# A written-out order replaced in a linear-attention and FFN kernel, with tiny copies placed between its loads

## The chip, the cores and the metric

One NeuronCore of one Trainium2 chip runs the program; the other cores are idle. The time is the device time of one execution in microseconds (us). An execution has five instruction streams: TensorE (PE; its weight loads are the row PEld), VectorE (DVE), ScalarE (ACT), GpSimd (POOL) and SyncE (SP), which here only issues transfers (DMAs). Each runs its own instructions in order and waits on semaphores for the others.

## What is computed

The first half is a chunked linear attention with decay over 4 batches, 8 heads, 768 tokens, head width 32 and state width 16; the second is a layer norm and a two-layer FFN (width 256, inner width 1024) with a residual.

```python
L = np.exp(cum[:, :, :, None] - cum[:, :, None, :]) * causal    # cum: running sum of log(a) in the chunk
y_intra = np.einsum('bhij,bhjd->bhid', (C B^T) * L, xc)
y_inter = np.einsum('bhin,bhnd->bhid', Cc, state) * np.exp(cum)[..., None]
state = decay_full * state + sum_j(B_j x_j * decay_from_j)
...
xn = (y - mean) / np.sqrt(var + 1e-06) * g_ln
out = y + np.maximum(xn @ w_ch1, 0.0) @ w_ch2
```

The weights arrive as 64-bit words and are turned into float32 on the chip, and then into an upper and a lower part of type fp32r, so that three fp32r products stand for one float32 product.

## The kernel before

The 768 tokens are cut into six blocks `t` of 128 tokens; a block holds all four batches, so a hidden tile has 512 columns. Every step of a block is a small function (a "layer"), called with the block and sometimes a group, half, batch or slice. The whole program is one list, `ISSUE` (from line 560): a text of short names with numbers, written out by hand or by a tool, in which each piece calls one function through the table `do` (line 543). The instructions of each engine run in the order of that list; a suffix (`:v`, `:a`, `:p`) puts a step on DVE, ACT or POOL, where the function's default would be another engine. Loads (`ld`) and stores (`od`) are all issued by SP in that order too. A buffer of a pool is given out in the order of the list, and the engine that writes it waits until the readers of its last content are done.

The names that matter here:

- Loads: `ld la` (the decays a), `ld sums`, `ld c t`, `ld b t`, `ld bt t`, `ld x t`, `ld as` (a in another layout), `ld g`, four quarters of W1 (`ld w1 c k`, 512 KB each: inner columns `c`, input rows `k`), four of W2 (`ld w2 c`), `ld mask`, `ld id`, `ld sel`.
- Decays of blocks 0 and 1: `l1`, `l2` (clip and logarithm), `e`, `x` (sums to the end of the chunk, exp), `lr`, `dc`, `du` (logarithms repeated, running sums on PE, exp into `u` and `d`), `so`, `sm`, `mb`, `sp`, `em` (sums of the sub-blocks, spread over the partitions).
- Decays of blocks 2 to 5: `rcl`, `ru`, `riv`, `rd` (two scans on DVE over `as`), `ro` (two writes of the result to a scratch tensor `scr` in HBM, line 322), `ld ud t` (loads of it, line 141).
- Attention of a block: `C`, `cx`, `cm` (C scaled and parted by head parity), `B` (B scaled), `ones` and `W` (mask and decays in `WW`), `G` (scores on PE, L375), `R` (scores times `WW`, L381), `be`, `Z`, `K`, `S`, `sb` (state of the half blocks), `c2`, `Vi` (product with the state, L394), `V` (product with x, L402), `y` (result to SBUF), `T`, `tc` (transposed), `yh`, `yl` (upper and lower part), `st`, `ag`, `rs`, `rc` (statistics).
- Weights: `k0` (ACT), `k1`, `k2`, `k3` (DVE), `kr` (ACT), `f` (sum of two integers, on POOL or DVE): words to float32; `gm` (centring matrix `gd`, `gneg` from g), `wc` (centring of W1 on PE, L230), `wh`, `wl` (upper and lower part).
- FFN: `h t m` (a hidden group, six products of 512 columns, L489), `hh` (relu and upper part), `hl` (lower part, DVE), `o t b` (24 products of 256 columns, L507), `oc 0 c j` (the same work of block 0 cut in four parts, L517), `oe` (scale and residual, DVE), `od` (store, 128 KB).
- `fill i n`: a product of zeros with n columns (L534), which computes nothing.

PSUM has eight banks: five for the attention (`ps_att`), three for `h`, `o`, `wc` and the sums (`ps_ffn`). Output tiles `o` come from a pool with three buffers. The hidden tiles `hh` and `hl` have nine buffers each.

```python
def load(what, *at, e=nc.sync):
    ...
    W1[at] = p1.tile([P, 1024], I32, tag=f"w1{c}{k}", name=f"raw1{c}{k}")
    e.dma_start(W1[at], w1v[k * P:(k + 1) * P, c * 1024:(c + 1) * 1024])
def finished(t, b):
    o = tiles["o", t, b] = p3.tile([P, DM], F32, tag="o", name=f"o{t}{b}")
for piece in ISSUE.split(","):
    name, *at = piece.split()
    name, _, engine = name.partition(":")
    do[name](*(int(v) if v.isdigit() else v for v in at), **({"e": engines[engine]} if engine else {}))
```

## Time and profile before

| what | value |
|---|---|
| median of 3 runs | 202.52 us (200.40 to 204.73) |
| profiled execution | 199.18 us |
| its span, first to last instruction | 197.4 us |
| mean granted TensorE clock | 0.998 |
| busy: PE, PEld, DVE, ACT, POOL | 188.8, 162.5, 129.1, 69.3, 35.7 us |
| HBM read, written | 14.74 MB, 3.28 MB |

The trace is one profiled execution; all its times are counted from the start of its span. The time of that execution holds 1.8 us more than the span. A busy engine is one with an instruction in it; products of PE are pipelined and their ends modelled, so a row's length can overlap the next row's. The view that follows the chain of work back from the last instruction shows one piece behind the other without overlap.

### The profile page before, as it was taken

The numbers are of one execution on the slowest core, as the hardware profiler recorded it, in microseconds if no ns is written. First come the engines' busy times: TensorE is split into PE (matmuls) and PEld (weight loads), VectorE is DVE, ScalarE is ACT, GpSimd is POOL, SyncE is SP. The second block draws the span as 40 slices with busy tenths as digits, with TensorE's granted clock in tenths as the row PEclk, the third lists the DMA queues.
The fourth block names the chain that finished last, engine by engine and source line by source line (L and its number), as shares of the span: only waits on it lengthen the run. The fifth ranks groups of instructions, "written<-read, shape, count | busy, mean of one in ns | idle before, by whom it ended". The sixth has DMA issues, their size and how long they took to land.

```text
span 197.4 us, 6404 instructions
## 1 busy us (share of the span) xinstructions
PE 188.8 (96%) x2854; PEld 162.5 (82%) x2854; DVE 129.1 (65%) x273; ACT 69.3 (35%) x127; POOL 35.7 (18%) x41
## 2 busy tenths in 40 slices
...
GB/s 118 286 367 401 375 307 235 202 149 15 3 163 0 0 53 119 220 67 58 3 3 0 3 150 67 3 3 0 11 72 53 0 3 3 80 27 3 19 17 71
DMA packets 11660, 18.42 MB, mean 93 GB/s; under 512 B 2385, under 2 KB 5873, under 8 KB 11633
## 3 DMA queue, kind: packets, MB, share of 16 engines
...
q8 instruction: 22, 0.36, 0.8%
...
HBM read 14.74 MB, written 3.28 MB: 91 GB/s over the span
## 4 chain that ended last, share of the span: by engine, by line
PE 90%; DVE 3%; ACT 3%; DMA 2%; issue 1%; POOL 0%; DVEq 0%
PE ph L489 32%; PE po L507 29%; PE pp L517 5%; PE yps L402 4%; PE wc L230 4%; PE G L375 4%; PE idle L534 4%; PE yps L394 3%; PE yt L458 3%; PE Z L414 2%; DMA out_dram<-o 2%; DVE hl L500 1%; DVE o L522 1%; ACT y L441 1%; PE cum L271 1%
## 5 line engine op out<-in xcount | busy, mean ns | idle before, releaser
L507 PE MATMUL po<-w,hh 128*128 128x256 f32 x320 | 56.8, 281 | 0.1
L489 PE MATMUL ph<-yh,w 128*128 128x512 f32 x192 | 53.8, 402 | 0.5 <-DVE hl L500 0.5
L507 PEld LDWEIGHTS po<-w,hh 128*128 128x128 f32 x320 | 49.1, 188 | 1.0 <-DVE hl L500 0.4
L507 PE MATMUL po<-w,hl 128*128 128x256 f32 x160 | 44.7, 279 | 0.0
L494 ACT ACTIVATE hh<-ph 128x512 fp32r<-128x512 f32 x34 | 20.2, 598 | 68.7 <-PE ph L489 59.8
L489 PEld LDWEIGHTS ph<-yh,w 128*128 128x128 f32 x192 | 34.3, 188 | 7.9 <-DVE hl L500 0.8
L500 DVE SCALAR_TENSOR_TENSOR hl<-ph,hh 128x512 fp32r<-128x512 f32 x48 | 32.3, 683 | 11.4 <-ACT hh L494 11.2
L507 PEld LDWEIGHTS po<-w,hl 128*128 128x128 f32 x160 | 30.1, 188 | 0.0
L489 PE MATMUL ph<-yl,w 128*128 128x512 f32 x96 | 29.8, 392 | 0.0
L522 DVE SCALAR_TENSOR_TENSOR o<-po,rstd,ytok 128x256 f32<-128x256 f32 x20 | 9.5, 480 | 27.3 <-PE po L507 27.2
L489 PEld LDWEIGHTS ph<-yl,w 128*128 128x128 f32 x96 | 18.0, 188 | 4.2 <-DVE yl L450 0.3
L381 DVE TENSOR_TENSOR R<-G,WW 128x512 f32<-128x512 f32 x24 | 15.7, 677 | 2.4 <-PE G L375 2.4
L450 POOL TENSOR_TENSOR yl<-y,yh 128x512 fp32r<-128x512 f32 x6 | 8.4, 1403 | 35.2 <-DVE yh L447 22.0
L496 DVE TENSOR_SCALAR hh<-ph 128x512 fp32r<-128x512 f32 x14 | 9.5, 681 | 4.9 <-PE ph L489 4.9
L441 ACT COPY y<-yps 128x256 f32<-128x256 f32 x15 | 5.2, 374 | 18.8 <-PE yps L402 15.1
L517 PE MATMUL pp<-w,hh 128*128 128x256 f32 x64 | 11.4, 281 | 0.0
L470 DVE BATCH_NORM_STATS2 st<-ytok 128x6 f32<-128x256 f32 x24 | 9.9, 416 | 1.4 <-ACT ytok L463 1.4
L517 PEld LDWEIGHTS pp<-w,hh 128*128 128x128 f32 x64 | 9.9, 188 | 0.3
L361 ACT COPY WW<-wt 32x1024 f32<-32x1024 f32 x8 | 8.3, 1040 | 5.1 <-DVE R L381 5.0
L534 PE MATMUL idle<-const-float32-0.0 128*128 128x128 f32 (+3 forms) x34 | 9.2, 425 | 0.8 <-PEq L624 0.8
L402 PE MATMUL yps<-R,xt 64*32 64x64 f32 x768 | 9.2, 226 | 0.0
L345 POOL TENSOR_TENSOR bs<-b,ud 128x512 f32<-128x512 f32 x3 | 3.9, 1293 | 28.6 <-DMA b<-in_bn_dram 28.6
...
## 6 DMA issues: line engine op xcount, KB each, us to landing
raw<-in_w_dram SPq DMA_DIRECT2D x8, 512.0 KB, 9.0
xt<-in_x_dram SPq DMA_DIRECT2D x6, 512.0 KB, 6.0
...
```

What stands on the lines that cost most here:

```text
L381: nc.vector.tensor_tensor(out=R.rearrange("p b i k -> p b (i k)"), in0=tiles.pop(("G", t, q)).rearrange("p b i k -> p b (i k)"), in1=WW.re ...
L402: nc.tensor.matmul(tiles["y", t, g, f][32 * k:32 * k + 32, b], x[r, b * NH + h], tiles["R", t, h // 2][r, b, h % 2], start=(t + f + b == 0 ...
L450: e.tensor_tensor(out=tiles["yl", t][:, g], in0=tiles["y32", t][:, g], in1=tiles["yh", t][:, g].bitcast(F32), op=ALU.subtract)
L470: nc.vector.bn_stats(out=st, in_=tiles["ytok", t][:, b])
L489: nc.tensor.matmul(ph, W1[m // 4, k][:, s, mc], v[:, k], start=(i == 0), stop=(i == len(cmb) - 1))
L494: e.activation(h, tiles["ph", t, m], AF.Relu)
L496: e.tensor_scalar(out=h, in0=tiles["ph", t, m], scalar1=0.0, scalar2=None, op0=ALU.max)
L500: nc.vector.scalar_tensor_tensor(out=l, in0=tiles.pop(("ph", t, m)), scalar=0.0, in1=tiles["hh", t, m].bitcast(F32), op0=ALU.max, op1=ALU. ...
L507: nc.tensor.matmul(po, tiles[v, t, m][:, cols], W2[m // 2,][:, s, (m % 2) * DM:(m % 2 + 1) * DM], start=(n == 0), stop=(n == len(cmb) - 1))
L517: nc.tensor.matmul(tiles["po", t, b], tiles[v, t, m][:, cols], W2[m // 2,][:, s, (m % 2) * DM:(m % 2 + 1) * DM], start=(c + n + b % 2 == 0 ...
L522: nc.vector.scalar_tensor_tensor(out=o, in0=tiles.pop(("po", t, b)), scalar=tiles["rstd", t][:, b], in1=tiles["ytok", t][:, b], op0=ALU.mu ...
L534: nc.tensor.matmul(ps[:, :n], zero.to_broadcast([P, P]), zero.to_broadcast([P, n]), start=True, stop=True)
```

## The change

Eight copies of 4 bytes (`pc`) are put between the loads. Each is issued by SP, reads the first element of a tile that is being loaded and writes it to a tile `seen` that nobody reads; so SP waits there until that load has landed. `gm`, a tile of g / 256, is left out, since `gneg` can be added instead of `gm` subtracted; the centring has a form for ACT, and so has `sb`. The output tiles get a pool of their own with six buffers, `rp` and `hp` one buffer more each. And the whole list `ISSUE` is a new one, with the same layers on the same data: 5 fills instead of 17; `ld w1 0 0` moved forward to fifth place, `ld as` and `ld g` moved back behind a copy; other engines for some steps (`be`, `c2`, `f` more often on POOL, `hh`, `y`, `yh`, `cm` more often on DVE, `sb` thrice on ACT, `ones` on POOL); and four hidden groups of block 0 (`h 0 1`, `0 2`, `0 0`, `0 3`) before the products `wc 1` of the second half of W1. The list is shown here by its opening in both versions, and by the end of the new one.

```diff
--- before.py
+++ after.py
@@ -88,8 +88,9 @@
     p1 = pool("p1", 1)
     p2 = pool("p2", 2)
     p3 = pool("p3", 3)
-    rp = pool("rp", 8)
-    hp = pool("hp", 9)
+    rp = pool("rp", 9)
+    hp = pool("hp", 10)
+    op = pool("op", 6)
 
     ov = out.rearrange("b (t p) f -> b t p f", p=P)
     w1v, w2v = w1.bitcast(I32), w2.bitcast(I32).rearrange("(m p) f -> p m f", p=P)
@@ -99,7 +100,6 @@
     cf = hp.tile([P, 4 * P], F32, tag="hl", name="cf")
     la = cp.tile([P, NT, NR], F32, name="la")
     gt = cp.tile([P, KC], F32, name="gt")
-    gm = cp.tile([P, KC], F32, name="gm")
     gneg = cp.tile([P, KC], F32, name="gneg")
     gd = hp.tile([P, KC, P], F32, tag="hh", name="gd")
     selt = cp.tile([NR, P + NB], F32, name="selt")
@@ -163,6 +163,13 @@
                 sums=(cf, coefs), g=(gt, g_ln), sel=(selt, sel))[what]
             e.dma_start(dst, src)
 
+    seen = cp.tile([1, 64], F32, name="seen")
+
+    def after(i, what, *at):
+        src = W1[at].bitcast(F32) if what == "w1" else W2[at].bitcast(F32) if what == "w2" else tiles[(what, *at)]
+        src = src.rearrange("p r d -> p (r d)") if what == "x" else src
+        nc.sync.dma_start(seen[:, 8 * i:8 * i + 1], src[:1, :1])
+
     epst = cp.tile([P, 1], F32, name="epst")
 
     def restart(e=nc.gpsimd):
@@ -218,11 +225,14 @@
         e.tensor_tensor(out=f, in0=f, in1=low.pop((w, *at)), op=ALU.add)
 
     def centring(e=nc.vector):
-
-        e.tensor_scalar(out=gm, in0=gt, scalar1=1.0 / DM, scalar2=None, op0=ALU.mult)
-        e.tensor_scalar(out=gneg, in0=gt, scalar1=-1.0 / DM, scalar2=None, op0=ALU.mult)
-        for k in range(KC):
-            e.tensor_scalar(out=gd[:, k], in0=ident, scalar1=gt[:, k:k + 1], scalar2=gm[:, k:k + 1], op0=ALU.mult, op1=ALU.subtract)
+        if e is nc.scalar:
+            e.activation(gneg, gt, AF.Copy, scale=-1.0 / DM)
+            for k in range(KC):
+                e.activation(gd[:, k], ident, AF.Identity, bias=gneg[:, k:k + 1], scale=gt[:, k:k + 1])
+        else:
+            e.tensor_scalar(out=gneg, in0=gt, scalar1=-1.0 / DM, scalar2=None, op0=ALU.mult)
+            for k in range(KC):
+                e.tensor_scalar(out=gd[:, k], in0=ident, scalar1=gt[:, k:k + 1], scalar2=gneg[:, k:k + 1], op0=ALU.mult, op1=ALU.add)
 
     def centred(c, k):
         w = centre[c, k] = ps_ffn.tile([P, 512], F32, tag="ffn", name=f"wc{c}{k}")
@@ -432,7 +442,12 @@
     def diagonal(t, f, e=nc.gpsimd):
 
         sb = tiles["sbd", t, f] = p2.tile([P, NB, 2 * HD], F32, tag=f"sbd{f}", name=f"sbd{t}{f}")
-        e.tensor_tensor(out=sb, in0=tiles[("S", *before(t, f))], in1=blkt.unsqueeze(1).to_broadcast([P, NB, 2 * HD]), op=ALU.mult)
+        S = tiles[("S", *before(t, f))]
+        if e is nc.scalar:
+            for i in range(2):
+                e.activation(sb[:, :, i * HD:(i + 1) * HD], S[:, :, i * HD:(i + 1) * HD], AF.Copy, scale=even[:, i:i + 1])
+        else:
+            e.tensor_tensor(out=sb, in0=S, in1=blkt.unsqueeze(1).to_broadcast([P, NB, 2 * HD]), op=ALU.mult)
 
     def gathered(t, g, f, e=nc.scalar):
         if ("y32", t) not in tiles:
@@ -518,7 +533,7 @@
                                  start=(c + n + b % 2 == 0), stop=(c == MC // 2 - 1 and b % 2 == 1 and n == len(cmb) - 1))
 
     def finished(t, b):
-        o = tiles["o", t, b] = p3.tile([P, DM], F32, tag="o", name=f"o{t}{b}")
+        o = tiles["o", t, b] = op.tile([P, DM], F32, tag="o", name=f"o{t}{b}")
         nc.vector.scalar_tensor_tensor(out=o, in0=tiles.pop(("po", t, b)), scalar=tiles["rstd", t][:, b], in1=tiles["ytok", t][:, b], op0=ALU.mult, op1=ALU.add)
 
     def stored(t, b):
@@ -541,7 +556,7 @@
 
     engines = {"s": nc.sync, "v": nc.vector, "p": nc.gpsimd, "a": nc.scalar}
     do = dict(
-        ld=load, fill=fill, fillb=fill_small, az=restart, ini=initial, inv=cleared, ones=masks, gm=centring,
+        ld=load, pc=after, fill=fill, fillb=fill_small, az=restart, ini=initial, inv=cleared, ones=masks, gm=centring,
         lr=logs_repeated, dc=since_middle, du=decay_from_middle, rcl=rest_clipped, ru=rest_since, riv=rest_last, rd=rest_till, ro=rest_out, C=scaled_c, cm=parted, cx=parted_at_once, B=scaled_b, c2=inter, be=ended,
         l1=clipped_a, l2=logs, e=sums_to, x=decays_to, so=sums_of, sm=decays_of, mb=apart, sp=spread, em=spread_copy,
         W=decays, G=score, R=weighted, Vi=entering, V=value, Z=carry, K=kept, S=state_of, sb=diagonal,
@@ -558,41 +573,41 @@
 
 
 ISSUE = """
-fill 0 128, az, ld la, fill 1 64, ld sums, fill 2 64, fill 3 128, ld mask, fill 4 64, ld as, fill 5 128, ld g, fill 6 64, l1, fill 7 128, inv,
-ld c 0, l2, ini, ld sel, lr 0, e 0, ld b 0, dc 0, x 0, ld id, ones, rcl, ld w1 0 0, ru, e 1, ld w1 0 1, du 0 0, riv, fill 8 512, rd, ld bt 0, lr 1,
-cx 0 0, ld x 0, du 0 1, cx 0 1, ld w1 1 1, x 1, so, ld c 1, B:v 0, dc 1, ld x 1, sm, W:v 0, ld w1 1 0, ld b 1, G 0, du 1 1, ld w2 0, mb, gm:p,
-ld w2 1, fill 9 256, R 0 2, ro 1, fill 10 128, ld bt 1, fill 11 128, R 0 0, fill 12 512, ld w2 2, k0 1 0 1, R 0 3, C 0, fill 13 64, k0 1 0 0, sp,
-fill 14 512, du 1 0, be:v 0, em 0, R 0 1, Z 0 0, k1 1 0 1, fill 15 256, S 0 0, c2 0, k0 1 1 1, k2 1 0 1, k1 1 0 0, kr 1 0 0, sb 0 1, kr 1 0 1,
-k2 1 0 0, Vi 0, C:v 1, V 0 0, k1 1 1 1, k3 1 0 0, fill 16 64, y 0 0 0, V 0 1, k3 1 0 1, y 0 0 1, cm 1 1, K 0 1, y 0 1 1, f:v 1 0 0, y 0 1 0,
-k0 1 1 0, T 0 0, f:v 1 0 1, T 0 1, cm 1 0, k1 1 1 0, wc 0 0, B:v 1, kr 1 1 1, k2 1 1 0, em 1, k2 1 1 1, kr 1 1 0, k3 1 1 0, ro 0, tc 0 0, wc 0 1,
-k3 1 1 1, ld bt 2, wh 1 0 0, ld c 2, f:v 1 1 0, tc 0 1, ld w2 3, yh:a 0 0, st 0 3, f 1 1 1, ld b 4, G 1, wh 1 0 1, ag 0 3, st 0 1, ld b 2, yh:a 0 1,
-ld c 4, be:v 1, Z 0 1, W 1, ld ud 2, wc 1 0, yl 0 1, S 0 1, ld x 2, wl:v 1 0 0, ld ud 4, wl:v 1 0 1, yl 0 0, k0 2 0, R 1 1, h 0 0, ld bt 3, k0 2 2,
-R 1 3, be 2, wh 1 1 0, R 1 0, kr 2 0, Z 1, R 1 2, sb 1 0, ld bt 4, hh 0 0, wl:v 1 1 0, K:p 1 0, h 0 1, W 2, k1 2 0, S 1 0, k2 2 0, wc 1 1, c2 1,
-hh 0 1, sb:v 1 1, k3 2 0, st 0 0, Vi 1, f:v 2 0, st 0 2, wh 2 0, V 1 0, ag 0 2, hl 0 0, wl 2 0, V 1 1, wh:v 1 1 1, y 1 0 1, hl 0 1, h 0 3, ld x 4,
-K:p 1 1, y:v 1 0 0, ag 0 0, wl:v 1 1 1, B 2, yh:a 1 0, h 0 7, y 1 1 1, S 1 1, k0 2 1, ag 0 1, y:v 1 1 0, C:v 2, rs 0, yh:a 1 1, h 0 5, k1 2 1,
-ld ud 3, hh 0 7, hh:v 0 3, yl 1 1, hl 0 7, Z 2, hh 0 5, hl 0 3, K:p 2 0, hl 0 5, T 1 1, c2:p 2, h 0 4, S 2 0, tc 1 1, cm 2 1, k1 2 2, yl:v 1 0,
-T 1 0, h 1 1, k2 2 1, tc 1 0, k3 2 1, kr 2 2, K 2 1, kr 2 1, h 1 5, st 1 0, rc 0, cm 2 0, sb:v 2 1, S 2 1, hh 0 4, C 4, G 2, hh 1 5, hl 0 4, hl 1 5,
...
+fill 0 512, ld la, ld sums, ld c 0, ld mask, fill 1 256, ld w1 0 0, l1, ini, ld b 0, l2, inv, ld sel, lr 0, e 0, dc 0, x 0, ld id, ones:p, du 0 1,
+ld bt 0, e 1, du 0 0, ld x 0, fill 2 64, lr 1, cx 0 0, x 1, dc 1, cx 0 1, k0 1 0 0, so, k1 1 0 0, du 1 1, C 0, du 1 0, sm, mb, B:v 0, W:v 0, G 0,
+pc 7 bt 0, ld g, ld w1 0 1, ld w1 1 1, pc 2 w1 0 0, ld as, ld w1 1 0, ld c 1, be 0, sp, em 0, kr 1 0 0, c2:p 0, k2 1 0 0, R 0 2, R 0 3, Z 0 0, R 0 1,
+Z 0 1, S 0 0, fill 3 64, az, k3 1 0 0, sb:a 0 1, fill 4 64, R 0 0, k0 1 0 1, f 1 0 0, Vi 0, kr 1 0 1, V 0 1, gm:a, W:p 1, k1 1 0 1, k2 1 0 1, V 0 0,
+y 0 1 0, y 0 0 0, y 0 0 1, pc 4 w1 1 0, ld c 2, pc 6 w1 1 1, ld bt 1, pc 1 x 0, pc 0 w1 0 1, ld b 1, y 0 1 1, ld bt 2, k0 1 1 1, pc 3 c 1, k0 1 1 0,
+K:p 0 1, k3 1 0 1, f:v 1 0 1, wc 0 0, yh 0 1, k1 1 1 1, ld x 1, wc 0 1, wh 1 0 0, ld w2 0, yl 0 1, yh 0 0, ld w2 1, em 1, ld w2 3, wh 1 0 1, T 0 1,
+yl 0 0, C:v 1, wl:v 1 0 0, rcl, S 0 1, T 0 0, wl:v 1 0 1, h 0 1, tc 0 0, be 1, K 1 0, h 0 2, c2:p 1, B:v 1, ru, hh 0 1, cm 1 1, cm 1 0, sb 1 0,
+k1 1 1 0, k2 1 1 1, riv, rd, h 0 0, hl 0 1, ro 1, kr 1 1 1, ld c 3, k2 1 1 0, ld b 3, k3 1 1 0, G 1, hh 0 0, ro 0, k3 1 1 1, kr 1 1 0, ld w2 2,
+f 1 1 1, h 0 3, R 1 1, k0 2 1, tc 0 1, R 1 2, hl 0 0, f 1 1 0, Z 1, ld ud 2, hh:v 0 2, wc 1 1, S 1 0, ld b 2, hl 0 2, sb:a 1 1, ld ud 3, R 1 0,
+hh 0 3, kr 2 1, R 1 3, wc 1 0, wh 1 1 1, wl:v 1 1 1, wh 1 1 0, hl 0 3, Vi 1, k0 2 0, wl:v 1 1 0, k1 2 1, V 1 1, K 1 1, C:v 2, V 1 0, y 1 1 1, k2 2 1,
+cm 2 0, h 0 5, k3 2 1, y 1 1 0, W 2, y:v 1 0 1, yh 1 1, h 0 6, S 1 1, cm:v 2 1, y:v 1 0 0, sb 2 0, h 0 7, kr 2 0, B 2, yl:v 1 1, hh 0 6, hh 0 5,
+be 2, k1 2 0, yh 1 0, st 0 3, ld b 4, G 2, hh 0 7, ld x 2, ld c 5, yl 1 0, f:v 2 1, hl 0 6, hl 0 5, T 1 1, h 1 7, hl 0 7, tc 1 1, K 2 0, R 2 2,
+T 1 0, hh:v 1 7, h 1 1, tc 1 0, st 0 0, kr 2 2, k2 2 0, k3 2 0, Z 2, hl 1 7, f 2 0, h 1 0, R 2 0, S 2 0, c2:p 2, R 2 1, h 0 4, hh 1 0, R 2 3, wh 2 1,
+sb 2 1, kr 2 3, Vi 2, K:p 2 1, C:v 3, hl 1 0, ld c 4, wh 2 0, ld bt 5, cm 3 0, wl:v 2 0, V 2 0, S 2 1, k0 2 3, V 2 1, wl:v 2 1, oc 0 0 0, ld x 3,
+k0 2 2, y:v 2 1 1, sb:v 3 0, ld ud 4, hh 1 1, ag 0 0, y:v 2 0 0, k1 2 2, oc 0 0 1, pc 5 x 1, ld bt 3, st 0 1, ld x 4, k2 2 2, cm:v 3 1, y:v 2 0 1,
+h 1 4, K 3 0, k3 2 2, st 1 1, f 2 2, oc 0 1 1, y:v 2 1 0, ag 0 3, hl 1 1, st 0 2, B 3, wh 2 2, oc 0 1 0, hh 0 4, hl 0 4, be 3, h 1 5, wl 2 2, k1 2 3,
+yh 2 1, hh:v 1 4, ld bt 4, h 1 2, hl 1 4, ag 0 1, st 1 0, ag 0 2, yl:v 2 1, h 1 6, k2 2 3, yh 2 0, k3 2 3, Z 3, st 1 2, f 2 3, hh:v 1 2, oc 0 2 1,
+yl 2 0, wh 2 3, oc 0 2 0, hh 1 5, c2:p 3, wl:v 2 3, ag 1 2, S 3 0, hl 1 2, oc 0 3 1, hh 1 6, ag 1 0, rs 0, C 4, rc 0, hl 1 5, oc 0 3 0, oe 0 3,
+K:p 3 1, oe 0 0, hl 1 6, h 1 3, ag 1 1, B:v 4, st 1 3, h 2 5, oe 0 2, hh 1 3, W 3, hl 1 3, h 2 1, hh:v 2 5, oe 0 1, S 3 1, od 0 1, cm 4 1, T 2 1,
+hh:v 2 1, ld b 5, o 1 3, ag 1 3, od 0 0, sb:v 4 0, rs 1, tc 2 1, be:v 5, ld ud 5, rc 1, hl 2 5, be:v 4, hl 2 1, o 1 1, G 3, T 2 0, R 3 1, B 5, o 1 0,
+tc:v 2 0, R 3 2, K:p 4 0, R 3 3, sb 3 1, c2:p 4, cm:v 4 0, R 3 0, Vi 3, oe 1 1, st 2 3, C 5, oe 1 0, st 2 2, h 2 3, ag 2 2, o 1 2, V 3 1, oe 1 2,
+cm:v 5 1, V 3 0, hh:v 2 3, y 3 1 0, Z 4, oe 1 3, y:v 3 0 1, od 1 3, h 2 2, y:v 3 0 0, od 0 3, c2 5, ld x 5, hl 2 3, od 1 2, h 2 4, S 4 0, hh 2 2,
...
+h 5 4, hh:v 5 3, hl 5 3, h 5 7, ag 5 2, hh:v 5 4, st 5 3, ag 5 0, hh:v 5 7, ag 5 3, hl 5 4, rs 5, hl 5 7, o 5 2, rc 5, o 5 0, oe 5 2, o 5 3, oe 5 0,
+od 5 0, od 1 0, od 4 0, od 3 2, od 4 2, o 5 1, od 5 2, oe 5 3, od 5 3, oe 5 1, od 5 1
 """
```

## Rows read from the trace of the kernel before

**Rows 1.** The page, busy time, share of the span and instructions of each engine
```profile
PE 188.8 (96%) x2854; PEld 162.5 (82%) x2854; DVE 129.1 (65%) x273; ACT 69.3 (35%) x127; POOL 35.7 (18%) x41
```

**Rows 2.** Table of stretches: length, busy us of PE, PEld, DVE, ACT, POOL; clock
```profile
15.00:17.50 2.50, 1.64 (x74) 1.17 (x77) 2.46 (x5) 2.18 (x4) 0.92 (x1) 1.00 1.02 410
...
45.00:50.00 5.00, 5.00 (x82) 3.88 (x81) 4.86 (x12) 4.48 (x8) 2.62 (x3) 1.00 0.02 5
...
75.00:80.00 5.00, 3.77 (x93) 2.75 (x79) 4.62 (x11) 1.08 (x2) 0.00 (x0) 1.00 0.61 189
...
180.00:197.40 17.40, 13.73 (x108) 13.09 (x106) 6.67 (x18) 1.33 (x3) 0.00 (x0) 0.98 0.10 32
```

**Rows 3.** The chain that ended last: start us, us, what
```profile
20.82 3.44 PE wc L230 x8
...
35.87 1.46 PE yps L402 x90
...
71.75 3.50 DMA out_dram<-o
...
147.15 8.18 PE ph L489 x36
...
182.53 11.21 PE po L507 x96
...
193.76 0.48 DVE o L522
```

**Rows 4.** Timeline of the opening: start us, us, engine, line, what
```profile
3.15 0.36 ACT L254 ACTIVATE la<-la 128x192 f32<-128x192 f32 x1 [1.14 <-DVE la L251]
...
5.41 1.06 ACT L181 COPY WW<-cst 128x1024 f32<-128x1024 f32 x1
...
6.37 0.60 ACT L277 ACTIVATE ud<-cum 128x512 f32<-128x512 f32 x1
...
7.00 1.42 DVE L341 SCALAR_TENSOR_TENSOR cm<-c,cst,ud 128x512 f32<-128x512 f32 x2 [1.02 <-ACT ud L277]
...
9.59 1.21 PE L375 MATMUL G<-cm,bs 32*64 32x128 f32 x64
...
10.82 1.89 DVE L381 TENSOR_TENSOR R<-G,WW 128x512 f32<-128x512 f32 x3 [0.42 <-PE G L375]
...
18.24 0.86 PE L402 MATMUL yps<-R,xt 64*32 64x64 f32 x64
```

**Rows 5.** DMA issues by line: KB each, median us from issue to landing
```profile
raw<-in_w_dram SPq DMA_DIRECT2D x8, 512.0 KB, 9.0
...
scr<-uds SPq DMA_DIRECT2D x2, 64.0 KB, 8.3
...
as<-in_as_dram SPq DMA_DIRECT2D x1, 64.0 KB, 2.4
```

**Rows 6.** Groups of POOL by line and form: busy us, mean ns
```profile
L450 POOL TENSOR_TENSOR yl<-y,yh 128x512 fp32r<-128x512 f32 x6 | 8.4, 1403 | 35.2 <-DVE yh L447 22.0 <-ACT yh L447 13.1
...
L422 POOL TENSOR_TENSOR K<-S,emt 128x256 f32<-128x256 f32 x4 | 2.5, 615 | 0.0
...
L363 POOL TENSOR_TENSOR WW<-wt,cst 128x1024 f32<-128x1024 f32 x1 | 1.9, 1922 | 5.9 <-DVE R L381 5.9
L218 POOL TENSOR_TENSOR top<-top,low 128x512 int32<-128x512 int32 x1 | 1.6, 1593 | 7.4 <-ACT ytok L463 7.4
...
L222 POOL TENSOR_SCALAR gm<-gt 128x2 f32<-128x2 f32 x1 | 1.2, 1199 | 0.0
```

**Rows 7.** Groups of DVE by line and form, a pass over 256 columns
```profile
L430 DVE TENSOR_TENSOR S<-Z,K 128x256 f32<-128x256 f32 x10 | 4.2, 415 | 1.2 <-PE Z L414 1.1
```

**Rows 8.** Timeline of SP's queue: the second write of decays, first load of them
```profile
17.45 0.78 SPq L322 DMA_DIRECT2D scr<-uds  x1
...
25.21 1.36 SPq L141 DMA_DIRECT2D ud<-scr  x2
```

32 lines of the change are left out of this document (11 added, 21 removed).

## The prediction

> **What bounds the kernel now.** I read the busy shares first, then the table of stretches, the chain of work that ended last, and only then the opening by instruction. TensorE (PE) is busy for 188.8 of 197.4 us, VectorE (DVE) for 129.1 [rows 1]. That alone would say "nothing to win", but PE's busy time holds filler products that compute nothing. The stretches show where PE works without a gap and where not: in 15 to 17.5 us it is busy 1.64 of 2.50 us; from 32.5 us on all stretches of that view read full, like 45 to 50, but for one, 75 to 80, with 3.77 of 5.00 [rows 2]. The chain is PE for almost its whole length: PE does the centring of W1 (`wc`) only from 20.82 to 24.26, and ends the attention of block 1 (its last `yps` piece) at 37.33. Once, at 71.75, it runs through 3.50 us of a store that holds an output buffer. The end is four `o` groups (11.21 us, 2.80 each), then one DVE addition and the last store [rows 3].
>
> So the bound has two parts: a start in which PE waits for loads and for DVE, and then PE's own work, which the change does not alter. Of real work PE does, in before, up to 37.3 us: all products of blocks 0 and 1 of the attention, all four `wc`, and two hidden groups (`h 0 0`, `h 0 1`). What matters is when the changed order has done the same, and whether PE is fed after that.
>
> **The opening, step by step.** The eight first fills (768 columns together) become two of 512 and 256, so the same columns; PE is free in time for the sums, since the logarithms are ready at 3.15 + 0.36 = 3.51 either way. Then `u` = exp(cum) is ready at about 6.7 instead of 6.97: the 1.06 us copy of the mask leaves ScalarE for GpSimd (POOL), and `lr 1` goes behind both exponentials. The two parted products take 1.42 us on DVE, so they end at about 8.15. The next DVE item is now a clamp of W1 (waits for `w1 0 0`), then `B 0`, whose load now stands behind that 512 KB; I put `B 0`'s end at 10.1 and `G 0` at 10.2, 0.6 us later than now (9.59) [rows 4].
>
> From there before loses time that the change saves. Today DVE does `B`, `W`, three `R`, then `be 0`, the last `R`, a clamp and `c2 0`; the last `V 0` ends at 19.10 (18.24 + 0.86). In the new order `be 0` and `c2 0` stand on POOL and the block mask `sb` on ACT. DVE then runs, after `B 0`, `W` to 11.7, one shift (0.4), three `R` in 1.89 to 14.0, a 0.7 us sign step and `R 0 0` to 15.3; POOL has `be 0` (about 10.8 to 11.9) and `c2 0` (to 13.0); `Z 0 0`, its copy and `sb` on ACT end near 13.6. So `Vi 0` and the first `V` run beside DVE, and the last `V 0` ends near 16.1: 3.0 us ahead [rows 4].
>
> Next is `wc 0`. It needs `w1 0 1`, which now is issued behind the first copy of 4 bytes. SP waits there until `bt 0` lands (I take 10.1); then the copy, `g` and `w1 0 1` go out, the last at 11.0. A load of 64 KB takes 2.4 us from issue to landing, a W1 quarter 9.0 in the crowded queue of today [rows 5]. These are the two ends for 512 KB, 2.4 to 9.0 us; I take 3.3, near the light end, because the copy has let the queue run empty: landing at 14.3. Then come magnitude (ACT) and four DVE passes (clamp, shift, sign, sum); at 0.63 a pass, the pace of the three `R` [rows 4], 3.1 us to 17.4, and both `wc 0` (3.44 us in the chain [rows 3]) end at about 20.0, against 24.3 today.
>
> What comes last before the first hidden group is then POOL: the sum of `w1 0 0` (1.59), `W 1` (1.92), `K 0 1` (0.62) and two `yl` (1.40 each) from 15.0 on, 1.59 + 1.92 + 0.62 + 2.80 = 6.9, so 21.9 [rows 6]. `h 0 1` ends at 22.4. `h 0 2`, `h 0 0` follow to 25.2, `G 1` to 26.3, `h 0 3` to 27.7, `Z 1` to 28.9; `wc 1` waits some for the two POOL sums of 1.59 and ends at 33.1; `Vi 1` and `V 1` add 2.5 and hand-over gaps 0.2: 35.8. By then four hidden groups are done, not two. A hidden group is 8.18 / 6 = 1.37 us (36 products [rows 3]). The opening is worth 37.3 - 35.8 + 2 x 1.37 = 4.2 us. Its bounds: 5.6 if no hand-over costs anything and `G 0` is not late; 1.0 if the loads behind the copies land 3 us later than I take.
>
> **The other edits.** The copies themselves: eight issues on SP, about 0.7 us each by the nearest rows (two `ud` loads in 1.36 [rows 8]), with nothing but later loads and stores behind them; they cost only through the loads, which is in the sum above. `gm` left out: 1.20 us of POOL [rows 6], which waited for nothing on the path: zero; the centring itself goes to ACT, three small passes that I bound between 0 and 1.8 (three at the 0.60 of a 512-column pass [rows 4]), beside `V 0`: zero. More output tiles (6 instead of 3): the wait of DVE for a store goes, and with it most of the hole of 5.00 - 3.77 = 1.23 us at 75 to 80 [rows 2, 3]; I take 1.2, bounds 0 and 1.7. One more `R` and one more hidden buffer: zero, between 0 and half a microsecond gained. Stores put off to the end: `od 1 0`, `4 0`, `3 2`, `4 2` stand between `od 5 0` and `od 5 2`, all issued while the last two `o` (5.6 us) run: zero, at most 1.
>
> **New waits.** From the end of `V 1` to `Z 3`, I counted the items of the new list. PE: 11 hidden groups (11 x 1.37 = 15.1), `G 2` 1.1, two `T 1` 0.9, `Z 2` and `Z 3` 2.3, `Vi 2` and `V 2` 2.5, four `oc` at half an `o` each 5.6: 27.5 us. DVE: 24 passes over 512 columns at 0.68, 29 over 256 at 0.42 [rows 7] and six short ones, 1.7: 30.2 us. Back to back, DVE passes come every 1.89 / 3 = 0.63 us where one takes 0.68 [rows 4], so DVE needs about 28.0 against 27.5. The old list, counted so from its `V 1` to its `Z 3`, has DVE 36.0 against PE 39.1. PE is no longer clearly the longer one, and every order with buffers of three leaves some unevenness: I take -0.8 us, bounds 0 and -4.
>
> **Sum.** 4.2 + 1.2 - 0.8 = 4.6 us off the profiled execution: span 192.8, that execution 194.6 instead of 199.18 (1.8 lies around the span, and 3.7 of the span behind PE's last product; both stay). The median of the runs shown is 202.52; the same 4.6 off it is 197.9, which is my forecast. A measurement of this kernel tells about 2%, 4.1 us, from no change, so the forecast is just beyond that.
>
> **A rule weighed.** The granted clock is 1.00 in every stretch up to 180 us, also in 15 to 17.5 where PE stands idle for a third, and 0.98 in the last, where PE has stopped [rows 2]. The Trainium skill, "TensorE: Matmul & The Clock Gate", Part 1, says that the slow clock is the default and that sustained activity releases it, so fewer fills (17 become 5) speak against this change. No row of before shows a fall during work. By the rule a hole that I expect before `wc 0` (16.1 to 17.4, less what of it starts early) could drop the clock; that is rival 3.
>
> **Rivals.**
> 1. *The lead is lost to DVE* (faster by 1 to 2 only). For it: the 28.0 against 27.5 above. Against it: before kept PE full from 45 to 50 us while DVE was busy for 4.86 of 5.00 [rows 2]. If DVE gives back 3 us: 4.2 + 1.2 - 3.8 = 1.6, so 200.9.
> 2. *The late decays stop DVE* (slower). `as` moves from fourth load to behind `w1 1 1`, so the two scans and the two writes `ro` come near 26 and 27 us instead of 14 and 17. `ud 2` must wait for these writes. Before, a write took 8.3 us to land [rows 5], the last was issued at 17.45 and `ud 2` at 25.21 [rows 8], well ahead of its reader. In the new order `C 2` stands on DVE at about 34.5; behind it queue the copies of `y 1`, `yl 1` and the `hl` of block 0, and PE has three hidden groups as cover, 4.1 us. With a light queue `ud 2` lands near 35 and costs under 1. With 8.3 us it is issued at 35.5 and lands near 39 to 40; if the second block of loads crowds it by 3 us more, DVE stands for 8 and PE for 8 - 4 = 4, and `B 2`, `cm 2` and `G 2` come later too, for 3 more. Then 4.2 + 1.2 - 0.8 - 7 = -2.4: 204.9. It decides from a landing of `ud 2` after about 41 us.
> 3. *The clock falls* in the gap before `wc 0`. The products of some 3.5 us after it (as long as `wc 0`) would take twice that: 4.6 - 3.5 = 1.1, so 201.4. By the rows of before, little chance.
> 4. *All hands over cleanly*: the opening at its upper bound and no new wait: 5.6 + 1.2 = 6.8, so 195.7.
> 5. *The copies do nothing*: the ring serves loads in order anyway, `w1 0 1` lands as late as the queue made it, only with the wait added. The opening falls to 1.5: 1.5 + 1.2 - 0.8 = 1.9, so 200.6.
>
> **Chances.** Forecast 0.52 (own range 195.5 to 200), rival 1 0.15, rival 2 0.10, rival 3 0.05, rival 4 0.12, rival 5 0.06. Faster by over 2% (under 198.5): all of rival 4 and three quarters of the forecast, 0.51. Slower by over 2%: half of rival 2 and mishaps of the others, 0.09. The rest, 0.40, is within 2%. The range leaves out the ends of rivals 2 and 4: 194.0 to 203.0.
>
> **What would show it.** In the changed profile: `V 0` ending near 16, `wc 0` starting near 17 and ending near 20, the first hidden group before 23, `V 1` ending near 36 with four hidden groups behind it; PE without a hole near 70 to 80; no DVE wait for a store. `w1 0 1` should land about 3.3 us after issue instead of 9. I am wrong if PE shows holes over 2 us between 35 and 65 us (rivals 1 or 2; the waits of `cs` for `ud` tell which), if the granted clock falls under 1 before 180 us (rival 3), or if W1's landing stays near 9 us (rival 5).

## The result and the profile after

The changed kernel takes 203.61 us (median of 20 runs), the kernel before 201.5 in the same comparison: ratio 1.015, interval 1.012 to 1.018. It is slower, where 197.9 and faster were forecast, and 0.6 us outside the range; the difference is under the 2% that the prediction takes as telling, but the interval leaves out 1. The ratios of this document leave out runs that are over 1.5% above the fastest of their kernel, and most of these are runs of the kernel before, so a ratio is larger than the quotient of the medians beside it. The profiled execution took 203.9 us with a span of 202.1, against 199.18 and 197.4.

The page after, busy time of each engine, answers to [rows 1]:

```profile
PE 188.1 (93%) x2830; PEld 161.0 (80%) x2830; DVE 140.0 (69%) x279; ACT 59.5 (29%) x113; POOL 51.0 (25%) x50
```

PE has as much as before. POOL rose by 15.3 us, which was planned. DVE rose by 10.9 us with six instructions more, which was not: its work lasts longer, as the groups of DVE below show. The table of stretches answers to [rows 2] (columns as there):

```profile
10.00:12.50 2.50, 0.16 (x8) 0.16 (x16) 2.50 (x3) 0.00 (x0) 1.74 (x3) 0.82 0.16 32
12.50:15.00 2.50, 2.50 (x66) 1.95 (x66) 1.76 (x3) 0.00 (x0) 0.00 (x0) 0.50 0.97 292
...
20.00:22.50 2.50, 2.50 (x90) 1.52 (x75) 2.32 (x3) 1.65 (x5) 1.32 (x2) 0.63 0.42 115
45.00:50.00 5.00, 2.79 (x73) 1.88 (x71) 5.00 (x6) 2.59 (x5) 3.93 (x3) 1.00 0.44 115
50.00:55.00 5.00, 4.04 (x55) 2.90 (x59) 4.96 (x10) 1.16 (x2) 0.30 (x1) 1.00 0.27 104
75.00:80.00 5.00, 4.79 (x37) 4.44 (x36) 4.04 (x10) 2.79 (x5) 4.04 (x4) 1.00 0.00 0
...
120.00:140.00 20.00, 19.49 (x383) 17.16 (x382) 14.05 (x31) 3.20 (x6) 1.92 (x1) 1.00 0.09 28
```

Three things stand here. The hole at 75 to 80 us is gone, as forecast. A new hole of 5.00 - 2.79 + 5.00 - 4.04 = 3.17 us is in 45 to 55, where before PE was full. And in 45 to 50 DVE is busy for all 5.00 us with 6 instructions, where before it did 12 in 4.86. The timeline, opening and that hole, answers to [rows 4]:

```profile
6.78 1.04 POOL L188 COPY WW<-cst 128x1024 f32<-128x1024 f32 x1 [6.34 <-DMA cst<-in_consts_dram]
...
7.05 1.99 DVE L351 SCALAR_TENSOR_TENSOR cm<-c,cst,ud 128x512 f32<-128x512 f32 x2 [3.67 <-ACT ud L287]
...
8.89 1.27 POOL L336 TENSOR_TENSOR cs<-c,ud 128x512 f32<-128x512 f32 x1 [1.06 <-ACT top L195]
8.96 1.48 DVE L200 TENSOR_SCALAR top<-top 128x512 f32<-128x512 f32 x1
...
10.12 0.60 POOL L301 TENSOR_TENSOR mblk<-msum,selt 32x144 f32<-32x144 f32 x1
10.37 1.92 DVE L355 TENSOR_TENSOR bs<-b,ud 128x512 f32<-128x512 f32 x1
...
10.69 1.05 POOL L364 TENSOR_TENSOR be<-bt,pend 128x512 f32<-128x512 f32 x1
...
12.34 2.01 PE L385 MATMUL G<-cm,bs 32*64 32x128 f32 x64 [3.12 <-DVE bs L355]
...
13.35 0.41 DVE L209 TENSOR_SCALAR top<-top 128x512 int32<-128x512 int32 x1
...
14.50 1.89 DVE L391 TENSOR_TENSOR R<-G,WW 128x512 f32<-128x512 f32 x3 [0.74 <-PE G L385]
...
15.49 1.05 POOL L359 TENSOR_TENSOR c<-cs,em 128x512 f32<-128x512 f32 x1 [3.75 <-ACT em L314]
...
18.47 2.09 POOL L373 TENSOR_TENSOR WW<-wt,cst 128x1024 f32<-128x1024 f32 x1
...
18.83 2.02 DVE L209 TENSOR_SCALAR top<-top 128x512 int32<-128x512 int32 x1
...
19.36 1.90 PE L412 MATMUL yps<-R,xt 64*32 64x64 f32 x114 [0.27 <-issue]
...
45.24 1.50 DVE L200 TENSOR_SCALAR top<-top 128x512 f32<-128x512 f32 x1
...
46.42 1.24 POOL L364 TENSOR_TENSOR be<-bt,pend 128x512 f32<-128x512 f32 x1
...
46.67 1.28 DVE L462 CAST yh<-y 128x512 fp32r<-128x512 f32 x1
...
48.03 1.26 POOL L465 TENSOR_TENSOR yl<-y,yh 128x512 fp32r<-128x512 f32 x1 [0.36 <-DVE yh L462]
48.20 1.63 DVE L225 CUSTOM_DVE_ANT_0 top<-top,low 128x1024 uint16<-128x1024 uint16 x1
...
49.76 1.87 DVE L515 SCALAR_TENSOR_TENSOR hl<-ph,hh 128x512 fp32r<-128x512 f32 x3
50.49 1.20 PE L504 MATMUL ph<-yh,w 128*128 128x512 f32 x4 [2.18 <-DVE hl L515]
```

Read the DVE rows beside the POOL rows. A shift (L209) takes 0.41 us at 13.35, when POOL stands still, and 2.02 us at 18.83, when it starts 0.36 us after the start of a POOL pass of 2.09 us: it ends at 20.85, 0.29 us after the POOL pass does. The clamp at 8.96, `bs` at 10.37 and the last sum at 48.20 show the same: each ends 0.28, 0.55 and 0.54 us after the POOL pass beside it. The three `R` at 14.50 read PSUM; `c2 0` runs on POOL beside them, and they take 1.89 us, as before [rows 4]. So some DVE passes don't run slowly beside POOL: they seem to stand until POOL's pass is over. Four groups of DVE by line and form show it in the mean; in before they are 490, 417, 416 and 684 ns, so by count and mean they last 7.6 us longer in all:

```profile
L200 DVE TENSOR_SCALAR top<-top 128x512 f32<-128x512 f32 x8 | 6.0, 744 | 0.2 <-ACT top L195 0.2
L209 DVE TENSOR_SCALAR top<-top 128x512 int32<-128x512 int32 x8 | 4.9, 613 | 0.0
L462 DVE CAST yh<-y 128x512 fp32r<-128x512 f32 x7 | 4.9, 695 | 0.0
...
L355 DVE TENSOR_TENSOR bs<-b,ud 128x512 f32<-128x512 f32 x3 | 4.1, 1372 | 0.0
```

The time by stages, from the ends of `V`: `V 1` ends at 41.66 (37.33 before) with two hidden groups more behind it, so the opening is worth 37.33 - 41.66 + 2 x 1.37 = -1.6 us (37.33 is 35.87 + 1.46 in the chain [rows 3]). From there to the end of `V 2` (59.43 + 1.48 = 60.91 after, 52.74 + 1.49 = 54.23 before) it takes 19.25 us with 7 hidden groups against 16.90 with 8: -2.35 - 1.37 = -3.7. The hole at 75 gives 4.79 - 3.77 = +1.0, and one at 120 to 140 takes 0.5. Together -4.8; the span grew by 4.7. The ends, in the timeline of the kernel before (`V 2`) and of that after (`V 1`, `V 2`):

```profile
52.74 1.49 PE L402 MATMUL yps<-R,xt 64*32 64x64 f32 x128
```
```profile
40.18 1.48 PE L412 MATMUL yps<-R,xt 64*32 64x64 f32 x128
...
59.43 1.48 PE L412 MATMUL yps<-R,xt 64*32 64x64 f32 x128
```

Four theories came out of this. *Holding*: DVE's passes wait for POOL's. *Clock*: the granted clock is 0.50 for some 10 us behind the gap before `G 0`. *Copies*: the loads are held back. *Order*: DVE's steps stand in the wrong order at 45 us.

### The profile page after: what moved, and what is told of

It reads as the page before. It is cut to its first block, busy times and chain, and to the rows that moved or that the text cites. A ratio compares the mean times of both kernels' runs of the same rounds, so it can differ in the third digit from the quotient of the medians.

```text
span 202.1 us, 6358 instructions
## 1 busy us (share of the span) xinstructions
PE 188.1 (93%) x2830; PEld 161.0 (80%) x2830; DVE 140.0 (69%) x279; ACT 59.5 (29%) x113; POOL 51.0 (25%) x50
## 4 chain that ended last, share of the span: by engine, by line
PE 66%; DVE 13%; DMA 9%; SPq 5%; issue 3%; POOL 2%; ACT 0%; POOLq 0%; DVEq 0%
PE po L522 28%; PE ph L504 25%; DMA bt<-in_bt_dram 5%; DMA raw<-in_w_dram 3%; PE yps L412 3%; PE yt L473 2%; PE yps L404 2%; DVE hl L515 2%; PE G L385 2%; SPq L171 2%; PE wc L240 2%; PE pp L532 1%; DVE w L249 1%; DVE yh L462 1%; DVE top L200 1%
## 5 line engine op out<-in xcount | busy, mean ns | idle before, releaser
L509 ACT ACTIVATE hh<-ph 128x512 fp32r<-128x512 f32 x25 | 14.7, 597 | 44.1 <-PE ph L504 31.4
L511 DVE TENSOR_SCALAR hh<-ph 128x512 fp32r<-128x512 f32 x23 | 15.6, 679 | 9.0 <-PE ph L504 5.7
L465 POOL TENSOR_TENSOR yl<-y,yh 128x512 fp32r<-128x512 f32 x8 | 10.7, 1349 | 40.6 <-ACT yh L462 37.5
L456 ACT COPY y<-yps 128x256 f32<-128x256 f32 x10 | 3.5, 374 | 43.5 <-PE yps L412 43.5
L225 POOL TENSOR_TENSOR top<-top,low 128x512 int32<-128x512 int32 x6 | 7.6, 1282 | 18.1 <-DVE top L214 14.2
L385 PE MATMUL G<-cm,bs 32*64 32x128 f32 x384 | 8.0, 302 | 3.7 <-DVE bs L355 3.1
L385 PEld LDWEIGHTS G<-cm,bs 32*64 32x64 f32 x384 | 6.4, 144 | 5.4 <-DVE bs L355 3.2
L412 PE MATMUL yps<-R,xt 64*32 64x64 f32 x768 | 10.1, 239 | 0.3 <-issue 0.3
```

The source lines that it names most:

```text
L385: nc.tensor.matmul(G[q][f * HALF:(f + 1) * HALF, b], bs[r, tok], cm[r, :, tok], start=True, stop=True)
L412: nc.tensor.matmul(tiles["y", t, g, f][32 * k:32 * k + 32, b], x[r, b * NH + h], tiles["R", t, h // 2][r, b, h % 2], start=(t + f + b == 0 ...
L465: e.tensor_tensor(out=tiles["yl", t][:, g], in0=tiles["y32", t][:, g], in1=tiles["yh", t][:, g].bitcast(F32), op=ALU.subtract)
L509: e.activation(h, tiles["ph", t, m], AF.Relu)
L511: e.tensor_scalar(out=h, in0=tiles["ph", t, m], scalar1=0.0, scalar2=None, op0=ALU.max)
```

## The experiments

The edits below are in the written order, unless said otherwise; the pieces shown are those that change.

**Copies.** Edit: all eight `pc` pieces removed (the copies alone; no output depends on them).

> The changed kernel without its eight copies of 4 bytes; the loads stand in the same order. Theory that SP's waits make loads late: w1 1 0, c 2, bt 1, b 1 and ud 2 go out earlier by 3 us and more and 2 to 4 us are won, about 200.5. Contention theory: DVE passes beside POOL stay long, the opening is as late as with the copies, and the time stays within 1 us of 203.6. If the copies do serve (they let early loads land alone), it gets slower by 1 us or more.

Measured: 203.32 us, ratio 1.018 (1.007 to 1.030). `G 0` starts at 12.01, `wc 0` at 21.07 (after: 12.34 and 21.19; the unedited control further down: 11.39 and 19.82). The copies neither cost nor bring anything that can be seen.

**Clock, first two tries.**

```diff
- B:v 0, W:v 0, G 0,
+ B:v 0, W:v 0, fill 10 512, fill 11 512, fill 12 512, G 0,
```

> The changed kernel with three filler products of 512 columns put back ahead of G 0 (3.1 us of filler in PE's gap of 3.5 us). Clock theory (the gap before G 0 drops the clock, and that makes the kernel slow): the granted clock stays at 1.00 from 10 to 22 us, and 2.5 to 4 us are won, about 200. Contention theory (DVE passes held up beside POOL make the kernel slow; the clock only stretches PE work that waits for DVE anyway): the clock stays at 1.00, G 0 still starts near 12.3 us, and 0 to 1 us is won, 202.6 to 203.6.

Measured: 203.55 us, ratio 1.026 (1.019 to 1.033): no gain. The profiled execution was the slowest of the four (208.94 us) and tells little, since the fills themselves ran at little over half speed (three in 5.49 us, where before needs 1.03 for one of that size) and pushed `G 0` to 16.67.

```diff
- fill 0 512, ld la, ... fill 2 64, lr 1, ... B:v 0, W:v 0, G 0,
+ fill 0 512, fill 10 128, fill 11 128, ld la, ... fill 12 512, lr 1, ... B:v 0, W:v 0, fill 13 512, fill 14 512, fill 15 256, G 0,
```

> The changed kernel with filler as in the kernel before: two products of 128 columns more at the start, so that PE runs on until the sums, one of 512 after them, and 1280 columns in the gap ahead of G 0; all other work as changed. Clock theory: each product runs at full clock from about 5 us, the granted clock stays at 1.00, and 2 us or more are won in the median, 201.6 or less. Contention theory: DVE's held passes still put G 0 at 12.3 and wc 0 at 22 us; at most 1 us is won; and if PE is still cold in the opening, the filler itself makes G 0 late and nothing or less than nothing is won.

Measured: 205.86 us, ratio 1.029 (1.016 to 1.041). The clock stood at 1.00 up to 17.5 us and was 0.62 and 0.70 after; nothing was won.

**Holding, in the opening.** POOL's passes beside DVE's chain go to ACT and DVE.

```diff
- ones:p, ... C 0, du 1 0, sm, mb, B:v 0, W:v 0, G 0, ... be 0,
+ ones, ... du 1 0, sm, mb, B:v 0, W:v 0, C:v 0, G 0, ... be:v 0,
```

> The changed kernel with POOL kept still until B 0 is done: the copy of the mask on ACT, C 0 and be 0 on DVE. Contention theory: the two cx passes take 1.42 us instead of 1.99, the clamp 0.42 instead of 1.48, B 0 0.68 instead of 1.92; G 0 starts near 10 us instead of 12.34; the clock stays at 1.00 because the gap is gone; 2 to 4 us are won in all, 200 to 201.5. Rival (the passes are long for another reason, the loads or the order): they stay long, G 0 stays after 11.5 us, and the time stays within 1 us of 203.6 or grows, since DVE gets 1.6 us more to do.

Measured: 202.88 us, ratio 1.025 (1.016 to 1.034). The durations came as the holding theory says: parted products 1.41, clamp 0.42, `bs` 0.68, `G 0` at 10.47. These alone prove little, since the unedited control further down has 1.42, 0.42 and 0.69 too. The shift, still beside `W 1` on POOL, took 2.02 us again. `V 2` ended at 60.43, half a microsecond ahead of after and 0.3 ahead of the control: hardly anything of an earlier `G 0` is left there.

Next, with `W 1` on ACT, and `f 1 0 0` and `K 0 1` on DVE as well:

```diff
- f 1 0 0, Vi 0, ... gm:a, W:p 1, ... K:p 0 1,
+ f:v 1 0 0, Vi 0, ... gm:a, W 1, ... K 0 1,
```

> The quiet start (mask copy on ACT, C 0 and be 0 on DVE), and further W 1 on ACT as in the kernel before, the sum of w1 0 0 and K 0 1 on DVE. That is some 1.1 us more for DVE by the rows and 2.1 us more for ACT. Contention theory: the second DVE shift (2.02 us beside W 1 on POOL) goes back to 0.42 and the sign pass (0.98) to 0.68, wc 0 starts and ends 0.5 to 2 us earlier than in the quiet start alone, V 1 ends near 38 to 39 us instead of 41.6; 201 to 202. Load theory (DVE and ACT have too much to do): the opening is no earlier than with the quiet start, 203 or more.

Measured: 203.09 us, ratio 1.018 (1.009 to 1.028). The shift takes 0.43 us now, with POOL still:

```profile
18.27 0.43 DVE L209 TENSOR_SCALAR top<-top 128x512 int32<-128x512 int32 x1
```

`V 1` ends at 40.57, 1.1 us ahead of after but level with the control (40.58). At 45 to 50 us PE is busy for 1.79 of 5.00 (after 2.79, control 2.38), and `V 2` ends at 60.62, 0.1 to 0.3 us ahead of the two.

**Holding, the other way round**: the kernel before, with three of its passes put on POOL where after has them. DVE is relieved of two of them, 1.6 us by the means of their groups (880 and 684 ns).

```diff
- be:v 0, em 0, ... S 0 0, c2 0, ... Z 0 1, W 1,
+ be 0, em 0, ... S 0 0, c2:p 0, ... Z 0 1, W:p 1,
```

> The kernel before, with three steps put on POOL as the change has them: be 0 and c2 0 from DVE, W 1 from ACT. By the rows this takes 1.6 us off DVE and 2.1 us off ACT in a stretch where DVE is full, and adds 4 us to POOL, which has room. If POOL's time were free (the prediction's reckoning), the opening is 0 to 1.5 us earlier, ratio to before 0.993 to 1.00. Contention theory: DVE passes beside the three POOL passes are held (W 1 alone for up to 1.6 us), DVE's busy time does not fall, and the kernel is 0.5 to 3 us slower, ratio 1.002 to 1.015.

Measured: 201.85 us, ratio 1.013 (1.004 to 1.021); DVE busy 129.8 against 129.1, although it has less to do. Timeline of this kernel:

```profile
12.76 1.28 POOL L326 TENSOR_TENSOR cs<-c,ud 128x512 f32<-128x512 f32 x1
...
13.80 1.54 DVE L193 TENSOR_SCALAR top<-top 128x512 f32<-128x512 f32 x1
14.00 1.05 POOL L354 TENSOR_TENSOR be<-bt,pend 128x512 f32<-128x512 f32 x1
15.02 1.23 POOL L349 TENSOR_TENSOR c<-cs,em 128x512 f32<-128x512 f32 x1
...
15.37 1.15 DVE L202 TENSOR_SCALAR top<-top 128x512 int32<-128x512 int32 x1
```

Clamp and shift, which took 0.49 and 0.42 us in the mean of before, stand beside `be` and `c2` here. Three passes on POOL alone made the kernel before slower, and nothing else of the change is in it. That DVE's passes are held is shown most plainly here. How much of the 1.3% is theirs is not separated, since a step moved to POOL also lasts longer itself: `c2` takes 1.23 us here and 0.68 on DVE in before.

**Holding, in the middle.**

```diff
- B 2, yl:v 1 1, ... be 2, k1 2 0, ... yl 1 0, f:v 2 1,
+ B:v 2, yl:v 1 1, ... be:v 2, k1 2 0, ... yl:v 1 0, f:v 2 1,
```

> The changed kernel with B 2, be 2 and yl 1 0 (44 to 50 us) on DVE instead of POOL. That is 2.2 us more work by the rows for DVE. Contention theory: the clamp (1.50), the cast (1.28) and the sum (1.63) that stood beside those POOL passes go back to about 0.42, 0.42 and 0.68, 2.9 us less; PE's hole at 45 to 50 us shrinks from 2.2 us by 0.5 to 1.5; 0 to 1.5 us are won. Load theory (DVE simply has too much to do there): the hole grows by up to 2.2 us and the kernel gets slower by 1 to 2 us.

Measured: 201.63 us, ratio 1.016 (1.010 to 1.022). Clamp, cast and sum last 0.41, 0.41 and 0.68 us, and DVE does 12 passes in 45 to 50 us instead of 6, although it got three more to do:

```profile
45.00:50.00 5.00, 3.33 (x75) 2.43 (x74) 5.00 (x12) 1.79 (x4) 0.00 (x0) 1.00 0.61 211
```

`V 2` ends at 59.00, 1.7 us ahead of the control. The opening is unedited here.

**Both together**, beside a control (the changed kernel with no edit) on the same chip:

> The changed kernel once more, with nothing edited, so that the two variants beside it have it on the same chip. Ratio to the kernel before as measured, 1.012 to 1.018; about 203.5 us. No theory differs here.

Measured: 203.84 us, ratio 1.019 (1.010 to 1.028).

> Changed kernel with every POOL pass that stood beside DVE's chain in the opening and around 45 us given to DVE or ACT (the quiet opening and the quiet middle together). Holding theory (passes of DVE wait for POOL's): the opening gains its 1 to 2 us, the hole at 45 to 55 us shrinks from 3 to about 2 us of idle PE, and the whole is 2.5 to 3.5 us under the control, 200.0 to 201.0. DVE-load theory (DVE simply has too much to do before 55 us, whoever waits for whom): the work given to it eats what the holding gave; not under the control by more than 1.5 us, no better than the quiet middle alone (201.6). In the trace: idle PE in 45 to 55 us over 2.5 us under the second theory.

Measured: 201.75 us, ratio 1.012 (1.008 to 1.016): 2.1 us under the control by the medians, less than the holding theory wanted, more than the load theory allowed. The control has four runs (201.64 to 204.14); by the two ratios it is some 1.5 us, and their intervals overlap, so the size is rough. Its table of stretches:

```profile
40.00:45.00 5.00, 5.00 (x83) 3.94 (x82) 5.00 (x12) 4.57 (x8) 0.82 (x1) 1.00 0.49 163
45.00:50.00 5.00, 2.83 (x15) 1.94 (x14) 5.00 (x11) 0.76 (x2) 0.00 (x0) 1.00 0.41 152
50.00:55.00 5.00, 5.00 (x90) 3.62 (x92) 4.97 (x10) 2.40 (x5) 3.79 (x4) 1.00 0.02 3
```

POOL stands still in 45 to 50 us, DVE's passes have their full pace, and PE still loses 2.17 us there: holding is not the whole cause there. In the opening "all quiet" is not quite quiet; three passes are still held beside POOL:

```profile
12.34 1.27 DVE L209 TENSOR_SCALAR top<-top 128x512 int32<-128x512 int32 x1
...
20.69 1.36 DVE L200 TENSOR_SCALAR top<-top 128x512 f32<-128x512 f32 x1 [0.27 <-ACT top L195]
...
25.40 1.53 DVE L355 TENSOR_TENSOR bs<-b,ud 128x512 f32<-128x512 f32 x1
```

**Clock, third try**, on top of all quiet:

```diff
- fill 0 512, ld la, ... fill 2 64, lr 1, ... C:v 0, G 0, ... R 0 2, R 0 3,
+ fill 0 512, fill 10 128, fill 11 128, ld la, ... fill 12 512, lr 1, ... C:v 0, fill 13 512, fill 14 256, G 0, ... fill 15 128, R 0 2, fill 16 128, R 0 3,
```

> As all quiet, with fills of 128 to 512 columns put before and between the first products of block 0. Clock theory (the granted clock of 0.5 to 0.6 in 12.5 to 22.5 us is what holds the opening): granted clock over 0.9 there, first wc over 1.5 us earlier than in all quiet, the whole over 1 us under all quiet. Holding or load theory: DVE sets these times; the same as all quiet within 0.7 us, or slower by the fills' own time before G 0.

Measured: 203.2 us, ratio 1.022 (1.013 to 1.030). Its table of stretches:

```profile
12.50:15.00 2.50, 2.50 (x74) 2.04 (x74) 2.50 (x6) 1.65 (x6) 1.12 (x3) 1.00 0.98 279
15.00:17.50 2.50, 1.18 (x64) 0.94 (x67) 2.47 (x6) 2.39 (x7) 0.00 (x0) 1.00 0.98 365
17.50:20.00 2.50, 2.29 (x127) 1.37 (x106) 1.43 (x3) 2.46 (x5) 0.00 (x0) 1.00 0.26 95
```

Here the clock was at 1.00 all through the opening (all quiet has 0.50 in 15 to 17.5; `G 0` takes 1.21 us in both, as in before), and the first `wc` started at 18.66 against 18.84, where the clock theory wanted 1.5 us. In 15 to 17.5 us PE works for 1.18 of 2.50: it waits for the other engines and spends the faster products idle. The whole is 1.45 us slower than all quiet. Fills that keep the clock up win nothing; what the lower clock itself costs isn't told apart from the fills' own time by this.

**Order.** Two DVE steps, `hl 0 6` and `hl 0 5`, that give PSUM back to PE's next hidden group, stand right behind their `hh`:

```diff
- yl:v 1 1, hh 0 6, hh 0 5, be 2, k1 2 0, yh 1 0, st 0 3, ... f:v 2 1, hl 0 6, hl 0 5, T 1 1,
+ yl:v 1 1, hh 0 6, hl 0 6, hh 0 5, hl 0 5, be 2, k1 2 0, yh 1 0, st 0 3, ... f:v 2 1, T 1 1,
```

> Changed kernel with two steps of DVE moved: hl 0 6 and hl 0 5, which free the PSUM tiles of h 0 6 and h 0 5, stand behind their hh instead of six DVE steps later (k1 2 0, yh 1 0, st 0 3, f 2 1 go behind them). Order theory (the hole at 45 to 50 us is the order of DVE's steps, whatever each lasts): PE's wait for hl (2.2 us) goes, idle PE in 45 to 55 us falls from 3.2 to under 1.5, the time falls by 1.5 to 2.0 us to some 201.8 (ratio to before about 1.009). Holding theory (DVE is late there because it is held beside POOL): what is put off is late in turn; PE waits as long for the yh, yl or f that now come last, and the time is within 0.7 us of the control's 203.8.

Measured: 201.98 us, ratio 1.016 (1.010 to 1.021); the span fell by 1.5 us to 200.6. Its waits of PE in the whole trace begin so:

```profile
PE yt L473 <- DVE R L391: 1.3, 1, 1.3
```

The wait of 2.2 us for `hl` is gone, as order says; idle PE in 45 to 55 us fell from 3.17 (control 2.62) to 2.08, not under 1.5, because PE then waits for an `R` that DVE reaches later, as holding says. In the trace each theory got half. In time the median is lower than after's, but the ratio of 1.016 isn't told from its 1.015.

The same on top of all quiet:

> All quiet with the same two steps moved. If holding and order are two separate costs: idle PE in 45 to 50 us falls from 2.2 to under 1.0 and the time from 201.75 to 199.8 to 200.5, level with the kernel before (ratio 1.000 to 1.006). If they are one cost: no gain over all quiet, 201.3 to 202.0. If the opening's gain of the prediction (4.2 us) were to be had at all, it would show here: 198 or less.

Measured: 202.13 us, ratio 1.018 (1.012 to 1.023): nothing over all quiet. The two costs do not add up, and neither mends the change.

**DVE's load.** All quiet with two DVE passes given to ACT, and its control:

```diff
- be:v 2, k1 2 0, yh 1 0, ... hh:v 1 7, h 1 1,
+ be:v 2, k1 2 0, yh:a 1 0, ... hh 1 7, h 1 1,
```

> All quiet once more with nothing else edited, as the control of the run beside it: about 201.7 us, 1.008 to 1.016 of the kernel before. No theory differs here.

> All quiet with two DVE passes between 43 and 50 us given to ACT: yh 1 0 (0.41 us) and hh 1 7 (0.67 us). DVE-bound theory (up to V 2 the time is DVE's busy time, since DVE has no gap from 10 us to there): V 2 ends 0.7 to 1.1 us earlier than in the control, idle PE in 45 to 55 us falls by as much, the time is 0.6 to 1.1 us under the control. Chain theory (PE waits there for one chain, hh to hl, and DVE's other work is beside it): V 2 and the time stay within 0.4 us.

Measured: 201.88 us (control, ratio 1.013, 1.005 to 1.022) and 201.61 us (1.012, 1.004 to 1.020). `V 1` to `V 2` takes 18.13 and 17.81 us. 0.3 us of 1.1 came: under what the load theory asks, and within the other's 0.4.

**Six output tiles alone**, on the kernel before, twice:

```diff
+    op = pool("op", 6)
-        o = tiles["o", t, b] = p3.tile([P, DM], F32, tag="o", name=f"o{t}{b}")
+        o = tiles["o", t, b] = op.tile([P, DM], F32, tag="o", name=f"o{t}{b}")
```

> The kernel before with six output tiles in a pool of their own, nothing else. The prediction's term: DVE's wait for a store at 72 to 75 us goes, PE's hole of 1.2 us at 75 to 80 us goes, 1.2 us are won, ratio 0.994. Rival: what waits at 75 us is the next hidden or state step, the hole stays or moves, and nothing is won, ratio 0.998 to 1.002.

Measured: 200.95 us in four runs too scattered for a ratio (196.41 to 202.03).

> Kernel before with six output tiles and nothing else, once more in more rounds. If the store wait was worth what the prediction gave it (1.2 us): 0.993 to 0.996 of the kernel before. If the wait was hidden anyway: 0.999 to 1.001. In the trace either way: DVE waits for no store, and PE is busy through 75 to 80 us.

Measured: 199.38 us, ratio 1.001 (0.996 to 1.006). Its row at 75 to 80 us:

```profile
75.00:80.00 5.00, 5.00 (x38) 4.74 (x39) 2.40 (x7) 0.00 (x0) 1.86 (x2) 1.00 0.82 248
```

The hole goes; the time doesn't show it. A gain of up to 0.7 us fits the interval, 1.2 does not.

All in one table, places from the profiled execution of each (us; idle PE is that in 45 to 55):

| kernel | `G 0` starts | `V 1` ends | `V 2` ends | idle PE | median |
|---|---|---|---|---|---|
| before | 9.59 | 37.33 | 54.23 | 0.00 | 201.5 |
| after | 12.34 | 41.66 | 60.91 | 3.17 | 203.61 |
| control | 11.39 | 40.58 | 60.74 | 2.62 | 203.84 |
| quiet opening | 10.54 | 40.57 | 60.62 | 3.86 | 203.09 |
| quiet middle | 10.17 | 40.87 | 59.00 | 2.13 | 201.63 |
| all quiet | 9.91 | 39.28 | 57.44 | 2.17 | 201.75 |
| early `hl` | 11.25 | 40.79 | 59.04 | 2.08 | 201.98 |
| all quiet, early `hl` | 9.75 | 39.86 | 58.18 | 2.33 | 202.13 |
| all quiet again | 10.12 | 39.97 | 58.10 | 2.14 | 201.88 |
| all quiet, two on ACT | 10.96 | 40.59 | 58.40 | 1.84 | 201.61 |

The rows have to be read with their spread. The changed opening stands unedited in after, control, quiet middle and early `hl`, and there `G 0` starts between 10.17 and 12.34 and `V 1` ends between 40.58 and 41.66. The quiet opening stands in five rows, with `V 1` between 39.28 and 40.59: in the mean 40.05 against 40.98, so it gains 0.9 us. `V 2` is steadier: 60.91 and 60.74 against 57.44 to 58.40 with both parts quiet. In the control no DVE pass ahead of `G 0` is held; POOL's `cs` stands beside DVE instead (2.19 us, 1.27 in after), and `G 0` comes behind PE's own running sums (`cum`), which take 1.92 and 2.08 us where after has 1.05 and 1.16. That is longer about as `G 0` is at a granted clock of 0.50 (2.01 in after, 1.21 in before), though the column reads 1.00 there:

```profile
5.04 1.92 PE L281 MATMUL cum<-cf,lr 128*128 128x128 f32 x8
...
8.11 1.42 DVE L351 SCALAR_TENSOR_TENSOR cm<-c,cst,ud 128x512 f32<-128x512 f32 x2 [4.64 <-ACT ud L287]
...
9.44 0.42 DVE L200 TENSOR_SCALAR top<-top 128x512 f32<-128x512 f32 x1
...
9.78 0.69 DVE L355 TENSOR_TENSOR bs<-b,ud 128x512 f32<-128x512 f32 x1
...
10.86 2.19 POOL L336 TENSOR_TENSOR cs<-c,ud 128x512 f32<-128x512 f32 x1 [4.26 <-issue]
...
11.39 1.67 PE L385 MATMUL G<-cm,bs 32*64 32x128 f32 x64
```

Medians come from different chips, too. Quiet middle and early `hl` have lower medians than after, but ratios of 1.016 where after has 1.015 and the control 1.019; what these two gain in time isn't settled.

## Why the prediction was wrong

**The step that failed** stands in the opening: "In the new order `be 0` and `c2 0` stand on POOL ... DVE then runs, after `B 0`, `W` to 11.7, one shift (0.4)", and at its start "the 1.06 us copy of the mask leaves ScalarE for GpSimd". What went to POOL was costed at zero for DVE, and DVE's passes were taken as they last alone (0.4 the shift, 0.63 a pass). Beside POOL such passes lasted 1.3 to 2.0 us. The prediction added up POOL's passes and DVE's apart; it never asked whether DVE and POOL can work at once. The Trainium skill, "SBUF — State Buffer", section "Who interferes with whom", states that DVE and GpSimd share one pair of ports as an exclusive lock: between a GpSimd pass that reads SBUF and a copy, cast or `tensor_scalar` of DVE in a two-port mode, or a DVE pass with two inputs in SBUF, the one that issues first keeps the pair for its whole length and the other stands. The trace agrees, with 2.02 us for a 0.41 us shift beside 2.09 us on POOL, and with the `R`, one input of which is in PSUM, at their old 1.89 for three. That rule stood against this change and was not weighed.

**The opening, +4.2 forecast, -1.6 measured** (-0.5 in the control, whose next stretch gives -4.6 instead of -3.7). `G 0` was put at 10.2 and came at 12.34, behind 3.12 us of waiting for the held `bs`. In other traces of the same opening it came at 11.39 with nothing held ahead of it, and at 10.17, so holding explains this delay but not every one. `V 1` was put at 35.8 and came at 41.66. The quiet opening has 40.05 in the mean, which is worth 37.33 - 40.05 + 2.74 = 0.0, and 39.28 at best, worth +0.8. So with these passes taken off POOL the loss goes, but no lead of 4.2 comes. What is left isn't free of holding: the three passes still held in all quiet last 2.7 us longer than the 0.41, 0.41 and 0.68 they take alone. The copies change nothing. Fills that kept the clock up won nothing; the quiet traces run from 39.28 with a granted clock of 0.83 in 10 to 20 us to 40.59 with 0.52, but not in step (40.57 with 0.74), so that a price of the lower clock, up to about a microsecond, is neither shown nor ruled out. DVE is busy for 9.61 of the 10 us from 10 to 20 in all quiet, for 9.45 in before. Where the rest of the 4.2 went is not shown.

**New waits, -0.8 forecast, -3.7 measured by the end of `V 2`.** The balance of 28.0 us on DVE against 27.5 on PE was drawn at free-standing durations, and as one sum over a long stretch. The loss is local, and part of it is holding (clamp, cast and sum at 45 to 50 us, 2.9 us longer than alone): seven hidden groups are done by 46 us, then PE has nothing that doesn't wait for DVE, which is full for 9.96 of the 10 us from 45 to 55. Rival 1 named a loss to DVE at 3.0 more; it took 2.9 more by `V 2`. That the sizes meet is partly luck, since the rival counted DVE's load and not its waiting for POOL. Its time of 200.9 failed because the opening that it rested on didn't come.

**Six output tiles, +1.2.** The hole went as said. In time the kernel before gains at most 0.7 us by it (the interval's lower end, 0.996): the term was mis-sized; where the rest of the 1.2 goes no run shows.

**The rivals.** 2 (late decays): `ud 2` was issued at 36.01, and `C 2` read it on DVE at 41.14 without a wait; not seen. 3 (clock): the clock did fall, to 0.50, behind the gap at 10 to 12.5 us. The Trainium skill, "TensorE: Matmul & The Clock Gate", Part 1, has the slow clock as the default and activity as what releases it; this row agrees. With the clock kept up by fills the time is no better, so nothing here shows the fall to be the main cause; a part of the loss may still be its. 4 didn't come. 5 (copies do nothing) is right about the copies, but the W1 and W2 pieces do land sooner, 4.3 us in the median against 9.0 [rows 5], and 5.7 without the copies, so mostly by the new order. `wc 0` didn't gain by it.

**What stays open.** Of the some 4.6 us between control and before on one chip (203.84 against 199.19), holding explains 2.1 by the medians of all quiet, some 1.5 by the ratios. The order of two DVE steps, alone, is worth 1.6 to 1.9 against the two medians of after, on other chips, nothing by its ratio, and nothing on top of all quiet. The other 2.5 us or more are not settled: DVE is busy for 45.55 of the 47.44 us from 10 us to the end of `V 2` in all quiet, which speaks for its load, but that includes the three held passes, and taking 1.1 us off it gave 0.3. No variant beats the kernel before; that with six output tiles is level with it.
